# Expert layer with w1 as the stationary operand, its last three tiles under a branch, and the routing moved inside the attention's branch

## The chip, the cores and the metric

The kernel runs on one core of one Trainium2 chip. The metric is device time in microseconds (us) of one execution. The core has a TensorE (PE for its matmuls, PEld for its weight loads), a VectorE (DVE), a ScalarE (ACT), a GpSimd (POOL) and a SyncE (SP); each runs its own instruction stream in order, and they tell each other of finished work by semaphores. A TensorE instruction multiplies a stationary operand, which is loaded first, with a moving operand that streams past it, and writes to PSUM.

## The reference, cut to what matters

A recurrent attention block gives x, one row of 384 values for each of 3072 tokens. Each token is then sent to one of eight experts, a two-layer network.

```python
logits = x @ w_gate                      # x: 3072 x 384, 8 experts
expert_idx = np.argmax(logits, axis=1)
gate_w = probs[np.arange(N), expert_idx] # softmax of the logits
for e in range(E):
    mask = expert_idx == e
    xe = x[mask]
    h = np.maximum(xe @ w1[e], 0.0)      # w1[e]: 384 x 1024
    ye = h @ w2[e]                       # w2[e]: 1024 x 384
    out[mask] = gate_w[mask, None] * ye
```

All of it is fp32. The inputs are drawn from a fixed seed. Counted over these inputs, the experts get 380, 348, 359, 410, 409, 389, 374 and 403 tokens; in tiles of 128 tokens of one expert that is 3 + 3 + 3 + 4 + 4 + 4 + 3 + 4 = 28 tiles.

## The kernel before, in words

**Attention.** L558 is a branch on the decay weights: `fast()` (L335 to L552), which these inputs take, or `general()` (L126 to L332). At its end `fast()` gates the last batch: `gate_step` and `choose` (L104) make the logits, write x of that batch to the HBM buffer `x_hbm` with a DMA from SP (L124), and leave a one-hot row per token in `oh_all` (L122). The program text of `general()` lies between `fast()` and what comes after the branch.

**Routing**, L571 to L653, after the branch. Two matmuls (L573, L574) and a chain of small DVE operations, which starts with copies out of PSUM (`rk` L578, `cnt` L579), give each token its rank in its expert, the expert `ei` of each tile (L622), and `idx` (L653), the token numbers of each tile. The number of tiles isn't known when the program is built, so the kernel always runs NTILE = 24 + 8 - 1 = 31 tiles; tiles past the real number gather a row of zeros, and their scatter drops every row.

**Experts**, L658 to L725. For a tile j there are five steps, in an order that is written out by hand:

- `m_load(j)`: PE and SP load the expert's number into a register (L660), SP starts the DMA of `w1` of that expert (1536 KB, L663, three buffers), POOL starts the gather of the tile's rows `xs` from `x_hbm` (L665, four buffers).
- `m_xT(j)`: three TensorE transposes (L673) of `xs`, copied out by DVE to `xT` (L675).
- `m_h(j)`: for each half `fb` of the 1024 hidden units three matmuls of 512 moving columns: a block of `xT` is stationary, `w1` is moving (L683); ACT takes the ReLU to `h` (L685), tokens on partitions.
- `m_hT(j)`: eight transposes of `h` (L694), copied out by DVE in two halves to `hT` (L695), hidden units on partitions.
- `m_y(j)`: eight matmuls of 384 moving columns (L701): a block of `hT` is stationary, `w2` of the expert is moving; DVE scales by the gate weight (L704), POOL starts the scatter to `out` (L705).

An fp32 matmul shows up in the profile as two passes, each with its own weight load: six matmuls in `m_h` are 12 PE instructions, eight in `m_y` are 16. A transpose is one pass.

The loop (L715 to L725) issues, for each j: load(j+2), h(j), y(j-1), xT(j+1), hT(j). So y of a tile runs one iteration after its h.

Of the kernel before, what the change touches and what calls it, by code (L numbers as in the profile page):

```python
# [32 lines left out]
NTILE = NG + E - 1  # L33

# [6 lines left out]
def rwkv5_then_switch(ctx, tc, r, k, ktm, v, w, wl, u, wg, wgh, w1, w2, out):  # L41
# [511 lines left out]

    for e in range(E):
        nc.scalar.dma_start(w2_all[:, e, :], w2[e])
    usual = nc.values_load(wi[0:1, 0:1], min_val=0, max_val=1,
                           skip_runtime_bounds_check_because="a product of two comparisons")
    with tc.If(usual > 0) as which:  # L558
        fast()
    with which.Else():  # L560
        general()


    mo = ctx.enter_context(tc.tile_pool(name="mo", bufs=2))
    rt = ctx.enter_context(tc.tile_pool(name="rt", bufs=1))
    pm = ctx.enter_context(tc.tile_pool(name="pm", bufs=1, space=PSUM))

    def small(shape, nm, dt=FP32):
        return rt.tile(shape, dt, name=nm)

    rkp = pm.tile([128, 512], FP32, name="rkp", tag="y", bufs=2)  # L571
    oh_f = oh_all.rearrange("p g e -> p (g e)")
    nc.tensor.matmul(rkp[:, 0:NG * E], lhsT=Tmat, rhs=oh_f, start=True, stop=True, skip_group_check=True)  # L573
    nc.tensor.matmul(rkp[:, 256:256 + NG * E], lhsT=ones_bf, rhs=oh_f, start=True, stop=True,  # L574
                     skip_group_check=True)
    rk = small([128, NG, E], "rk")
    cnt = small([128, NG, E], "cnt")
    nc.vector.tensor_copy(rk.rearrange("p g e -> p (g e)"), rkp[:, 0:NG * E])  # L578
    nc.vector.tensor_copy(cnt.rearrange("p g e -> p (g e)"), rkp[:, 256:256 + NG * E])  # L579
    inc = cnt  # L580
    d = 1
    while d < NG:
        t = small([128, NG, E], f"inc{d}")
        nc.vector.tensor_copy(t[:, 0:d], inc[:, 0:d])
        nc.vector.tensor_tensor(t[:, d:], inc[:, d:], inc[:, :NG - d], op=ALU.add)
        inc = t
        d *= 2

    nc.vector.tensor_tensor(rk, rk, inc, op=ALU.add)
    nc.vector.tensor_tensor(rk, rk, cnt, op=ALU.subtract)  # L590
    nc.vector.tensor_tensor(rk, rk, oh_all, op=ALU.mult)
    rank = small([128, NG], "rank")
    nc.vector.tensor_reduce(rank, rk, axis=AX, op=ALU.add)
    rki = small([128, 3, NG], "rki", I32)
    nc.vector.tensor_copy(rki[:, 0, :], rank)
    nc.vector.tensor_scalar(out=rki[:, 1, :], in0=rki[:, 0, :], scalar1=127, scalar2=None, op0=ALU.bitwise_and)
    nc.vector.tensor_scalar(out=rki[:, 2, :], in0=rki[:, 0, :], scalar1=7, scalar2=None,
                            op0=ALU.logical_shift_right)
    rlh = small([128, 2, NG], "rlh")
    nc.vector.tensor_copy(rlh, rki[:, 1:3, :])  # L600

    ci = small([128, E], "ci", I32)
    nc.vector.tensor_scalar_add(ci, inc[:, NG - 1, :], 127.0)
    nc.vector.tensor_scalar(out=ci, in0=ci, scalar1=7, scalar2=None, op0=ALU.logical_shift_right)
    til = small([128, E], "til")
    nc.vector.tensor_copy(til, ci)
    last = til
    for d in (1, 2, 4):
        t = small([128, E], f"til{d}")
        nc.vector.tensor_copy(t[:, 0:d], last[:, 0:d])  # L610
        nc.vector.tensor_tensor(t[:, d:], last[:, d:], last[:, :E - d], op=ALU.add)
        last = t
    base = small([128, E], "base")
    nc.vector.tensor_tensor(base, last, til, op=ALU.subtract)

    tge = small([1, NTILE, E], "tge")
    nc.vector.tensor_tensor(tge, bc(iota_f[0:1, 0:NTILE, None], [1, NTILE, E]),
                            bc(last[0:1, None, :], [1, NTILE, E]), op=ALU.is_ge)
    ef = small([1, NTILE], "ef")
    nc.vector.tensor_reduce(ef, tge, axis=AX, op=ALU.add)  # L620
    ei = small([1, NTILE], "ei", I32)
    nc.vector.tensor_scalar_min(ei, ef, float(E - 1))  # L622

    nc.vector.tensor_tensor(rk, oh_all, bc(base[:, None, :], [128, NG, E]), op=ALU.mult)
    jt = small([128, NG], "jt")
    nc.vector.tensor_reduce(jt, rk, axis=AX, op=ALU.add)
    nc.vector.tensor_tensor(jt, jt, rlh[:, 1, :], op=ALU.add)

    At = small([128, NG, 128], "At", BF16)
    nc.vector.tensor_tensor(At, bc(iota_f[:, None, :], [128, NG, 128]),  # L630
                            bc(rlh[:, 0, :, None], [128, NG, 128]), op=ALU.is_equal)
    Bm = small([128, NG, NTILE], "Bm")
    nc.vector.tensor_tensor(Bm, bc(iota_f[:, None, 0:NTILE], [128, NG, NTILE]),
                            bc(jt[:, :, None], [128, NG, NTILE]), op=ALU.is_equal)
    hi_f = small([128, NG], "hi_f")
    nc.vector.tensor_scalar_add(hi_f, iota_f[:, 0:NG], 1.0)
    Bv = small([128, NG, 2, NTILE], "Bv", BF16)
    nc.vector.tensor_tensor(Bv[:, :, 0, :], Bm, bc(hi_f[:, :, None], [128, NG, NTILE]), op=ALU.mult)
    nc.vector.tensor_scalar_mul(Bv[:, :, 1, :], Bm, lo_f)
    idp = pm.tile([128, 2, NTILE], FP32, name="idp", tag="y", bufs=2)  # L640
    for g in range(NG):
        nc.tensor.matmul(idp.rearrange("p u j -> p (u j)"), lhsT=At[:, g, :],
                         rhs=Bv[:, g].rearrange("p u j -> p (u j)"), start=g == 0, stop=g == NG - 1)
    idl = small([128, 2, NTILE], "idl")
    nc.vector.tensor_copy(idl, idp)
    emp = small([128, NTILE], "emp")
    nc.vector.tensor_scalar(out=emp, in0=idl[:, 0, :], scalar1=0.0, scalar2=float(N + 128),
                            op0=ALU.is_equal, op1=ALU.mult)
    raw = small([128, NTILE], "raw")
    nc.vector.scalar_tensor_tensor(out=raw, in0=idl[:, 0, :], scalar=128.0, in1=idl[:, 1, :],  # L650
                                   op0=ALU.mult, op1=ALU.add)
    idx = small([128, NTILE], "idx", I32)
    nc.vector.scalar_tensor_tensor(out=idx, in0=raw, scalar=-128.0, in1=emp, op0=ALU.add, op1=ALU.add)  # L653


    mt = [dict() for _ in range(NTILE)]

    def m_load(j):  # L658
        m = mt[j]
        m["e"] = nc.values_load(ei[0:1, j:j + 1], engines=[ENG.PE, ENG.SP], min_val=0, max_val=E - 1,  # L660
                                skip_runtime_bounds_check_because="a count of at most E, cut to E - 1")
        m["w1"] = mo.tile([128, DT, F], FP32, name="w1s", bufs=3)
        nc.sync.dma_start(m["w1"], w1[ds(m["e"], 1)].rearrange("a p d f -> p (a d) f"))  # L663
        m["xs"] = mo.tile([128, W], FP32, name="xs", bufs=4)
        nc.gpsimd.indirect_dma_start(  # L665
            out=m["xs"], out_offset=None, in_=x_hbm[:, :],
            in_offset=bass.IndirectOffsetOnAxis(ap=idx[:, j:j + 1], axis=0))

    def m_xT(j):
        m = mt[j]  # L670
        p = pm.tile([128, DT, 128], FP32, name="xTp", tag="xT", bufs=1)
        for d in range(DT):
            nc.tensor.transpose(p[:, d, :], m["xs"][:, 128 * d:128 * d + 128], ident)  # L673
        m["xT"] = mo.tile([128, DT, 128], FP32, name="xT", bufs=2)
        nc.vector.tensor_copy(m["xT"], p)  # L675

    def m_h(j):
        m = mt[j]
        m["h"] = mo.tile([128, F], FP32, name="h", bufs=2)
        for fb in range(2):  # L680
            p = pm.tile([128, 512], FP32, name="hp", tag="h", bufs=3)
            for d in range(DT):
                nc.tensor.matmul(p, lhsT=m["xT"][:, d, :], rhs=m["w1"][:, d, fb * 512:(fb + 1) * 512],  # L683
                                 start=d == 0, stop=d == DT - 1)
            nc.scalar.activation(m["h"][:, fb * 512:(fb + 1) * 512], p, func=ACT.Relu)  # L685

    def m_hT(j):
        m = mt[j]
        m["hT"] = mo.tile([128, FT, 128], FP32, name="hT", bufs=2)
        for fb in range(2):  # L690
            p = pm.tile([128, 4, 128], FP32, name="hTp", tag="hT", bufs=2)
            for f in range(4):
                o = (4 * fb + f) * 128
                nc.tensor.transpose(p[:, f, :], m["h"][:, o:o + 128], ident)  # L694
            nc.vector.tensor_copy(m["hT"][:, 4 * fb:4 * fb + 4, :], p)  # L695

    def m_y(j):
        m = mt[j]
        p = pm.tile([128, DM], FP32, name="yp", tag="y", bufs=2)
# [11 lines left out]
    with tc.manual_schedule():  # L711
        for j in range(2):
            m_load(j)
        m_xT(0)
        for j in range(NTILE + 1):  # L715
            if j + 2 < NTILE:
                m_load(j + 2)
            if j < NTILE:
# [54 lines left out]
```

## Time and profile before

| | us |
|---|---|
| median of 3 runs | 602.97 (601.86 to 608.3) |
| the profiled execution, its own time | 607.18 |
| its span, first to last instruction | 605.5 |
| PE busy in the span | 516.7 |
| weight loads (PEld) busy | 340.0 |
| DVE, ACT, POOL busy | 182.5, 129.4, 161.0 |

The page also says that 96.48 MB went by DMA, 159 GB/s on average. Attention takes the first 204 us, routing some 30 us with TensorE nearly idle, the expert loop the rest. The mean duration of one PE instruction is longer than the distance between two, since matmuls are pipelined; the distance between starts is what a pass costs in a stream.

### The profile page before, as it was taken

The numbers are of one execution on the slowest core, as the hardware profiler recorded it, in microseconds if no ns is written. First come the engines' busy times: TensorE is split into PE (matmuls) and PEld (weight loads), VectorE is DVE, ScalarE is ACT, GpSimd is POOL, SyncE is SP. The second block draws the span as 40 slices with busy tenths as digits, with TensorE's granted clock in tenths as the row PEclk, the third lists the DMA queues.
The fourth block names the chain that finished last, engine by engine and source line by source line (L and its number), as shares of the span: only waits on it lengthen the run. The fifth ranks groups of instructions, "written<-read, shape, count | busy, mean of one in ns | idle before, by whom it ended". The sixth has DMA issues, their size and how long they took to land.

```text
span 605.5 us, 8757 instructions
## 1 busy us (share of the span) xinstructions
PE 516.7 (85%) x3223; PEld 340.0 (56%) x3223; DVE 182.5 (30%) x442; ACT 129.4 (21%) x379; POOL 161.0 (27%) x185
## 2 busy tenths in 40 slices
PE   0029898998997206999999999999999999999996
PEld 0028887998896202555555555555555555555553
DVE  6115767337443260211311221131122113112211
ACT  0026675445564000010011001001101100110110
POOL 5038875445560011111211121121112112111101
PEclk9999999569799556999999999999999999999999
DMA  7998654933922253645444544544454454455000
GB/s 263 355 335 206 170 147 123 208 79 110 210 54 79 84 232 133 224 141 206 159 152 162 203 145 145 206 148 150 169 186 153 145 192 161 145 175 191 29 0 0
DMA packets 22295, 96.48 MB, mean 159 GB/s; under 512 B 4352, under 2 KB 7462, under 8 KB 17252
## 3 DMA queue, kind: packets, MB, share of 16 engines
q1 hardware_dynamic: 17124, 72.40, 36.9%
q0 software_dynamic: 3968, 10.84, 5.7%
q10 hardware_dynamic: 1152, 12.58, 5.6%
q8 instruction: 29, 0.48, 0.3%
q14 instruction: 22, 0.18, 0.1%
HBM read 86.36 MB, written 10.83 MB: 161 GB/s over the span
## 4 chain that ended last, share of the span: by engine, by line
issue 57%; PE 19%; DMA 8%; POOL 7%; DVE 6%; ACT 3%; ACTq 0%; POOLq 0%; DVEq 0%; SPq 0%
DMA w_all<-in_moe_w_dram 6%; POOL xs L665 5%; PE rp L513 4%; PE P L447 4%; PE yp L504 3%; PE P L453 3%; PE yp L500 2%; POOL out_dram L705 2%; ACT A L461 2%; PE Gp L478 2%; DMA x_hbm<-xb 1%; DVE A L463 1%; DVE St L485 1%; DVE At L630 1%; DMA V<-in_v_dram 1%
## 5 line engine op out<-in xcount | busy, mean ns | idle before, releaser
L683 PE MATMUL hp<-w1s,xT 128*128 128x512 f32 x372 | 170.0, 607 | 0.7 <-DVE xT L675 0.7
L701 PE MATMUL yp<-w_all,hT 128*128 x496 | 165.1, 486 | 0.4 <-DVE hT L695 0.4
L701 PEld LDWEIGHTS yp<-w_all,hT 128*128 128x128 f32 x496 | 94.2, 190 | 72.5 <-issue 14.3
L683 PEld LDWEIGHTS hp<-w1s,xT 128*128 128x128 f32 x372 | 68.9, 192 | 82.7 <-issue 75.4
L705 POOL DMA_INDIRECT out_dram<-yo,idx x31 | 31.5, 1015 | 306.4 <-DVE yo L704 296.5
L685 ACT ACTIVATE h<-hp 128x512 f32<-128x512 f32 x62 | 37.0, 597 | 349.8 <-PE hp L683 349.8
L704 DVE TENSOR_SCALAR yo<-yp,xs 128x384 f32<-128x384 f32 x31 | 19.2, 618 | 289.4 <-PE yp L701 289.4
L461 ACT ACTIVATE A<-ident,dv 128x128 f32<-128x128 f32 x192 | 59.6, 389 | 0.1
L428 POOL TENSOR_TENSOR K<-kT,W 128x384 f32<-128x384 f32 x32 | 36.1, 1127 | 67.7 <-DMA kT<-in_k_dram 29.4
L463 DVE COPY_PREDICATED A<-mask,P 128x384 f32<-128x384 int32 x64 | 33.9, 583 | 57.2 <-ACT A L461 48.7
L447 PE MATMUL P<-R,K 48*128 48x128 f32 x384 | 35.2, 324 | 18.4 <-POOL K L428 14.3
L665 POOL DMA_INDIRECT xs<-x_hbm,idx x31 | 30.4, 980 | 55.5 <-issue 55.5
L504 PE MATMUL yp<-A,V 128*64 128x128 f32 x384 | 43.7, 305 | 1.2 <-DVE A L463 1.1
L447 PEld LDWEIGHTS P<-R,K 48*128 48x128 f32 x384 | 28.4, 218 | 23.6 <-POOL K L428 14.9
L695 DVE COPY hT<-hTp 128x512 f32<-128x512 f32 x62 | 39.6, 680 | 0.0
L500 PE MATMUL yp<-R,St 128*64 128x128 f32 x320 | 36.1, 306 | 0.0
L513 PE MATMUL rp<-IW,y 128*128 128x104 f32 x192 | 32.2, 319 | 4.0 <-DVE lg L516 4.0
L432 POOL TENSOR_TENSOR RK<-rT,kT 128x384 f32<-128x384 f32 x32 | 34.2, 1068 | 0.1
L513 PEld LDWEIGHTS rp<-IW,y 128*128 128x128 f32 x192 | 27.6, 222 | 8.8 <-DVE lg L516 4.9
L694 PE MATMUL hTp<-ident,h 128*128 128x128 f32 x248 | 32.3, 273 | 0.0
L504 PEld LDWEIGHTS yp<-A,V 128*64 128x64 f32 x384 | 27.9, 156 | 1.6 <-DVE A L463 1.6
L453 PEld LDWEIGHTS P<-wu,RK 48*128 48x128 f32 x384 | 28.7, 219 | 0.0
(111 smaller groups left out, 313.1 us busy)
## 6 DMA issues: line engine op xcount, KB each, us to landing
w1s<-in_moe_w_dram SPq DMA_DIRECT2D x31, 1536.0 KB, 6.4
w_all<-in_moe_w_dram ACTq DMA_DIRECT2D x8, 1536.0 KB, 20.0
x_hbm<-xb SPq DMA_DIRECT2D x4, 1155.0 KB, 5.8
rT<-in_r_dram SPq DMA_DIRECT2D x32, 144.0 KB, 3.9
kT<-in_k_dram SPq DMA_DIRECT2D x32, 144.0 KB, 3.9
kt<-in_k_tokens_dram SPq DMA_DIRECT2D x16, 288.0 KB, 4.7
V<-in_v_dram SPq DMA_DIRECT2D x16, 288.0 KB, 4.0
xs<-x_hbm,idx POOLq DMA_INDIRECT x31, 3.1
```

The costliest lines, as they stand in the source:

```text
L447: nc.tensor.matmul(P[hi][:, c * C:(c + 1) * C], lhsT=x["K"][q, c, :], rhs=x["R"][q, c, :], start=True, stop=True, skip_group_check=True)
L453: nc.tensor.matmul(P[hi][:, o:o + 1], lhsT=x["RK"][q, c * C:(c + 1) * C], rhs=wu[q, 1, hp:hp + 1], start=True, stop=True, skip_group_check ...
L461: nc.scalar.activation(A[:, hi, c, :], ident, func=ACT.Copy, scale=dv[:, hi, c:c + 1])
L463: nc.vector.copy_predicated(A[:, hi], bc(mask[:, None, :].bitcast(I32), [128, HC, C]), P[hi][:, 0:HC * C].rearrange("p (c t) -> p c t", c=HC))
L500: nc.tensor.matmul(yp[q, c, :], lhsT=m["St"][:, g, hi, :], rhs=x["R"][:, c, :], start=True, stop=False, skip_group_check=True)
L504: nc.tensor.matmul(yp[q, c, :], lhsT=vh(x, c, hi, 64), rhs=x["A"][:, hi, c, :], start=g == 0, stop=True, skip_group_check=True)
L513: nc.tensor.matmul(rp[:, hp, :], lhsT=pairs[b * HP + hp]["y"][:, ch * C:(ch + 1) * C], rhs=IW[:, hp, :], start=True, stop=True, skip_group ...
L665: nc.gpsimd.indirect_dma_start(out=m["xs"], out_offset=None, in_=x_hbm[:, :], in_offset=bass.IndirectOffsetOnAxis(ap=idx[:, j:j + 1], axis=0))
L683: nc.tensor.matmul(p, lhsT=m["xT"][:, d, :], rhs=m["w1"][:, d, fb * 512:(fb + 1) * 512], start=d == 0, stop=d == DT - 1)
L695: nc.vector.tensor_copy(m["hT"][:, 4 * fb:4 * fb + 4, :], p)
L701: nc.tensor.matmul(p, lhsT=m["hT"][:, f, :], rhs=w2_all[:, ds(m["e"], 1), f * DM:(f + 1) * DM], start=f == 0, stop=f == FT - 1)
L705: s_ = nc.gpsimd.indirect_dma_start(out=out[:, :], out_offset=bass.IndirectOffsetOnAxis(ap=idx[:, j:j + 1], axis=0), in_=y[:, :], in_offse ...
```

## The change

1. **w1 stationary.** In `m_h` a 128x128 block of `w1` is now the stationary operand and `xT` (128 columns) the moving one. The product comes out with hidden units on partitions, so the ReLU writes `hT` directly; `m_hT` is gone, and `h` with it. Three matmuls for each of eight blocks: 24 matmuls of 128 columns in place of 6 of 512.
2. **Order.** For each j: load(j+2), h(j), xT(j+1), y(j).
3. **Tile count.** NSURE = 24 + 4 = 28 tiles are run always; the other three lie under `tc.If(tiles > NSURE)`, where `tiles` is the real count, loaded into a register on each engine.
4. **Seam.** Routing and experts are a function `experts()` that is called inside each arm of the branch of L558, after `fast()` and after `general()`, not once behind it.

Cut to its core (the routing's lines move with no other change than `nt`):

```diff
+NSURE = NG + E // 2
...
+        nt = small([1, 1], "nt", I32)
+        nc.vector.tensor_copy(nt, last[0:1, E - 1:E])
...
+        tiles = nc.values_load(nt[0:1, 0:1], min_val=0, max_val=NTILE,
+                               skip_runtime_bounds_check_because="at most NTILE tiles by their count")
...
+        def m_h(j):
+            m = mt[j]
+            m["hT"] = mo.tile([128, FT, 128], FP32, name="hT", bufs=2)
+            for fb in range(2):
+                p = pm.tile([128, 4, 128], FP32, name="hp", tag="h", bufs=4)
+                for f in range(4):
+                    o = (4 * fb + f) * 128
+                    for d in range(DT):
+                        nc.tensor.matmul(p[:, f, :], lhsT=m["w1"][:, d, o:o + 128], rhs=m["xT"][:, d, :],
+                                         start=d == 0, stop=d == DT - 1)
+                nc.scalar.activation(m["hT"][:, 4 * fb:4 * fb + 4, :], p, func=ACT.Relu)
...
+        with tc.manual_schedule():
+            for j in range(2):
+                m_load(j)
+            m_xT(0)
+            for j in range(NSURE):
+                if j + 2 < NTILE:
+                    m_load(j + 2)
+                m_h(j)
+                if j + 1 < NTILE:
+                    m_xT(j + 1)
+                m_y(j)
+        with tc.If(tiles > NSURE):
+            with tc.manual_schedule():
+                for j in range(NSURE, NTILE):
...
     with tc.If(usual > 0) as which:
         fast()
+        experts()
     with which.Else():
         general()
...
+        experts()
...
-    def m_h(j):
-        m = mt[j]
-        m["h"] = mo.tile([128, F], FP32, name="h", bufs=2)
-        for fb in range(2):
-            p = pm.tile([128, 512], FP32, name="hp", tag="h", bufs=3)
-            for d in range(DT):
-                nc.tensor.matmul(p, lhsT=m["xT"][:, d, :], rhs=m["w1"][:, d, fb * 512:(fb + 1) * 512],
-                                 start=d == 0, stop=d == DT - 1)
-            nc.scalar.activation(m["h"][:, fb * 512:(fb + 1) * 512], p, func=ACT.Relu)
-
-    def m_hT(j):
...
-                nc.tensor.transpose(p[:, f, :], m["h"][:, o:o + 128], ident)
-            nc.vector.tensor_copy(m["hT"][:, 4 * fb:4 * fb + 4, :], p)
...
-        for j in range(NTILE + 1):
-            if j + 2 < NTILE:
-                m_load(j + 2)
-            if j < NTILE:
-                m_h(j)
-            if j > 0:
-                m_y(j - 1)
-            if j + 1 < NTILE:
-                m_xT(j + 1)
-            if j < NTILE:
-                m_hT(j)
```

## Rows read from the trace of the kernel before

**Rows 1.** The page's 40 slices of the span: PE busy, granted clock.
```profile
PE   0029898998997206999999999999999999999996
PEclk9999999569799556999999999999999999999999
```

**Rows 2.** The page's group of hT's transposes: count | busy us, mean ns | idle before.
```profile
L694 PE MATMUL hTp<-ident,h 128*128 128x128 f32 x248 | 32.3, 273 | 0.0
```

**Rows 3.** Windows of one expert tile: us, PE busy (instructions), clock, DMA share, GB/s.
```profile
242.64:247.86 5.22, 5.22 (x14) 1.00 0.68 275
247.86:253.02 5.16, 5.16 (x17) 1.00 0.79 288
253.02:254.36 1.34, 1.34 (x12) 1.00 0.16 64
254.36:583.42 329.06, 329.06 (x1094) 1.00 0.44 155
```

**Rows 4.** Timeline, PE and PEld, 128x128 blocks stationary: start us, us, what.
```profile
77.79 1.14 PE L513 MATMUL rp<-IW,y 128*128 128x104 f32 x8
77.79 0.97 PEld L513 LDWEIGHTS rp<-IW,y 128*128 128x128 f32 x8 [0.17 <-issue]
115.31 1.78 PEld L513 LDWEIGHTS rp<-IW,y 128*128 128x128 f32 x8 [0.33 <-issue]
253.35 1.04 PE L694 MATMUL hTp<-ident,h 128*128 128x128 f32 x8
78.86 0.94 PE L447 MATMUL P<-R,K 48*128 48x128 f32 x12
```

**Rows 5.** Line L513's weight loads: count, ns min/median/max, first to last start us.
```profile
L513 PEld LDWEIGHTS rp<-IW,y x192: 186/192/338, 77.8 to 200.6; 128*128 128x128 f32 x192
```

**Rows 6.** Timeline of the last tile's end.
```profile
594.57 1.28 DVE L695 COPY hT<-hTp 128x512 f32<-128x512 f32 x2
595.30 5.43 PE L701 MATMUL yp<-w_all,hT 128*128 x16 [0.43 <-DVE hT L695]
600.77 0.62 DVE L704 TENSOR_SCALAR yo<-yp,xs 128x384 f32<-128x384 f32 x1 [4.92 <-PE yp L701]
```

**Rows 7.** Timeline of ACT in the expert loop, one ReLU.
```profile
248.06 0.60 ACT L685 ACTIVATE h<-hp 128x512 f32<-128x512 f32 x1 [1.98 <-PE hp L683]
```

**Rows 8.** Timeline from the end of attention to the first expert matmuls.
```profile
203.71 0.21 DVE L122 TENSOR_TENSOR oh_all<-eq,m 128x48 bf16<-128x48 f32 x1
204.18 0.36 PE L574 MATMUL rkp<-oh_all,ones_bf 128*128 128x192 bf16 x1
209.58 0.36 DVE L578 COPY rk<-rkp 128x192 f32<-128x192 f32 x1 [5.66 <-DMA x_hbm<-xb]
...
225.23 1.18 POOL L665 DMA_INDIRECT xs<-x_hbm,idx  x1 [46.31 <-issue]
...
233.93 7.50 PE L683 MATMUL hp<-w1s,xT 128*128 128x512 f32 x12 [0.65 <-DVE xT L675]
```

**Rows 9.** Single lines' sequencer instructions: count, ns min/median/max, first to last start us.
```profile
L558 DVEq COMPARE_BRANCH  x2: 50/54/57, 4.3 to 203.7; - x2
L558 ACTq COMPARE_BRANCH  x2: 38/42/45, 11.3 to 202.5; - x2
L578 DVEq EVENT_SEMAPHORE  x5: 21/50/50, 207.8 to 209.5; - x5
L685 ACTq EVENT_SEMAPHORE  x5: 17/38/29463, 205.1 to 209.4; - x5
L769 POOLq DRAIN  x3: 45/113/3185, 601.4 to 605.2; - x3
L769 SPq DRAIN  x3: 7/7/13, 604.4 to 604.9; - x3
```

**Rows 10.** Windows, all engines: PE, PEld, DVE, ACT, POOL busy, clock, DMA, GB/s.
```profile
100.00:200.00 100.00, 89.75 (x1108) 82.58 (x1105) 47.95 (x136) 50.87 (x174) 41.54 (x45) 0.80 0.47 120
```

**Rows 11.** DMA issues: engine, operation, count, KB each, median us to landing.
```profile
w1s<-in_moe_w_dram SPq DMA_DIRECT2D x31, 1536.0 KB, 6.4
```

More of the change, by code (lines that the diff above doesn't have):

```diff
@@ L559, in rwkv5_then_switch @@
         fast()
+        experts()
     with which.Else():
         general()
[L564 to L652, printed above, removed]
@@ L653, in rwkv5_then_switch @@
-    nc.vector.scalar_tensor_tensor(out=idx, in0=raw, scalar=-128.0, in1=emp, op0=ALU.add, op1=ALU.add)
-    mt = [dict() for _ in range(NTILE)]
-    def m_load(j):
-        m = mt[j]
[L660 to L667, printed above, removed]
@@ L669, in m_xT @@
-    def m_xT(j):
-        m = mt[j]
-        p = pm.tile([128, DT, 128], FP32, name="xTp", tag="xT", bufs=1)
-        for d in range(DT):
-            nc.tensor.transpose(p[:, d, :], m["xs"][:, 128 * d:128 * d + 128], ident)
-        m["xT"] = mo.tile([128, DT, 128], FP32, name="xT", bufs=2)
-        nc.vector.tensor_copy(m["xT"], p)
-    def m_h(j):
-        m = mt[j]
-        m["h"] = mo.tile([128, F], FP32, name="h", bufs=2)
-        for fb in range(2):
-            p = pm.tile([128, 512], FP32, name="hp", tag="h", bufs=3)
-            for d in range(DT):
-                nc.tensor.matmul(p, lhsT=m["xT"][:, d, :], rhs=m["w1"][:, d, fb * 512:(fb + 1) * 512],
-                                 start=d == 0, stop=d == DT - 1)
-            nc.scalar.activation(m["h"][:, fb * 512:(fb + 1) * 512], p, func=ACT.Relu)
@@ L687, in m_hT @@
-    def m_hT(j):
[L688 to L693, printed above, removed]
-                nc.tensor.transpose(p[:, f, :], m["h"][:, o:o + 128], ident)
-            nc.vector.tensor_copy(m["hT"][:, 4 * fb:4 * fb + 4, :], p)
-    def m_y(j):
-        m = mt[j]
-        p = pm.tile([128, DM], FP32, name="yp", tag="y", bufs=2)
-        for f in range(FT):
-            nc.tensor.matmul(p, lhsT=m["hT"][:, f, :], rhs=w2_all[:, ds(m["e"], 1), f * DM:(f + 1) * DM],
-                             start=f == 0, stop=f == FT - 1)
-        y = mo.tile([128, DM], FP32, name="yo", bufs=3)
-        nc.vector.tensor_scalar_mul(y, p, m["xs"][:, DM:W])
-        s_ = nc.gpsimd.indirect_dma_start(
-            out=out[:, :], out_offset=bass.IndirectOffsetOnAxis(ap=idx[:, j:j + 1], axis=0),
-            in_=y[:, :], in_offset=None, bounds_check=N - 1, oob_is_err=False)
-        tc.declare_no_dep(s_.ins, group="sc", reason="each token stands in one tile: the rows are disjoint")
-        tc.add_to_no_dep_group("sc", s_.ins)
@@ L711, in rwkv5_then_switch @@
[L711 to L714, printed above, removed]
-        for j in range(NTILE + 1):
-            if j + 2 < NTILE:
-                m_load(j + 2)
-            if j < NTILE:
-                m_h(j)
-            if j > 0:
-                m_y(j - 1)
-            if j + 1 < NTILE:
-                m_xT(j + 1)
-            if j < NTILE:
-                m_hT(j)
+        experts()
 _INS = ['r', 'k', 'k:tokens', 'v', 'w', 'w:row', 'u', 'moe_w_gate', 'moe_w_gate:heads', 'moe_w1', 'moe_w2']
```

123 lines of the change are left out of this document (added).

## The prediction, as put on record

> **What bounds the kernel now.** I read the page's slices first [rows 1]: PE is busy at 0.9 and more from slice 16 on, at full clock, to the end; before it comes a hole of two slices (0 and 2) in which the routing runs. So there are two things to shorten: the expert loop, where PE is the limit, and the hole, where a chain on other engines is. The page's groups then show what in the loop could go: 248 transposes of `hT`, eight for each of 31 tiles, 32.3 us of PE, none of it idle time [rows 2]. The windows of one tile [rows 3] give its parts: h 5.22 us, y 5.16, the three xT and eight hT transposes with their boundary 1.34, in sum 11.72; the last row holds 28 tiles from h to h, 329.06 / 28 = 11.752 us each, PE busy all of it at clock 1.00. Thirty-one of these are 364.3 us of the 605.5 us span. No DMA, ACT or DVE time matters in the loop as long as it is under that.
>
> **h with w1 stationary.** The product is the same, and so is the number of moving columns: 12 passes of 512 before, 48 of 128 after. Before, a pass costs 5.22 / 12 = 0.435 us, so 128 columns are 0.109 us. What is new is a weight load for each 128 columns, not for each 512. The attention stage holds the nearest rows. In L513 each fp32 pass has its own 128x128 stationary block and 104 moving columns; at full clock eight loads take 0.97 us [rows 4], the last of them 0.192 [rows 5], so one pass follows another after (0.97 - 0.192) / 7 = 0.111 us. The 104 columns alone would take 0.109 x 104/128 = 0.089 and leave no room for a load beside them in series: load and moving operand overlap, and the load sets the pitch. The transposes with 128 moving columns [rows 2, 4] give (1.04 - 0.273) / 7 = 0.110. A group of eight L513 passes including the switch to the next line (77.79 to 78.86) takes 1.07 us: 0.18 us for the switch, which after the change comes once in 48 passes. I take 0.111: h costs 48 x 0.111 = 5.33 us, 0.11 more than before. The bounds are 0.109 (the columns alone) and, if nothing were hidden, 0.220 (a rival, below).
>
> The Trainium skill speaks against this edit: its page "TensorE: Matmul & The Clock Gate", Back-to-back issue gap, gives 81 ns for a load-and-matmul pair of 128 columns where the matmul alone would take 56. By that ratio a pass here would be an estimated 0.158 us, h 7.6, and the sum about 606 us, no gain. The rows of L513, 0.111, do not show that ratio.
>
> **hT gone.** Eight transposes leave PE. Of the 1.34 us of xT and hT [rows 3], 11 x 0.110 = 1.21 are transposes and 0.13 is a boundary wait. Three transposes, 0.33, stay. Two DVE copies a tile go too, worth nothing since DVE is covered by PE.
>
> **Tile period after.** h 5.33 + xT 0.33 + y 5.16 + 0.14 for boundaries (about what is lost now) = 10.96 us.
>
> **Order.** y(j) now follows its own h after only three transposes. The last ReLU of a tile starts 0.20 us after the next PE work starts (247.86 against 248.06) and takes 0.60 [rows 3, 7], so it ends 0.80 us after h; the transposes cover 0.33. But y begins with the blocks f = 0 to 3, which the first ReLU wrote some 2.6 us earlier, and these passes last 2.6 us. It needs that the halves of `hT` are waited for separately. They are: y of the last tile starts at 595.30, 0.73 after the two copies began, while the second runs on to 595.85 [rows 6]. Cost 0. If the cover were gone, see the first rival. xT(j+1) is copied by DVE under the 5.16 us of y. On POOL the gather of j+2 now stands ahead of the scatter of j, on SP only w1 loads stand; the gather's buffer was freed two tiles before. A w1 load needs 6.4 us [rows 11] and is issued as soon as h(j-1) is done, 3 x 10.96 - 5.3 = 27.5 us ahead of its use. PE's register load per tile is unchanged and runs ahead of the array.
>
> **Three tiles less.** The reference's own inputs make 28 tiles, and 28 > 28 is false: the branch skips the last three. Loop: 31 x 11.752 = 364.3 before, 28 x 10.96 = 306.9 after: -57.4. The drain of the last tile (y waits 0.43 for its own `hT` [rows 6]) goes: -0.4. The start stays: the first 12 passes take 7.50 us [rows 8], 2.3 over 5.22, because PE comes cold from the hole, and it will again. Two loads of w1 that nobody uses (tiles 28, 29) lie under the last two tiles.
>
> **Seam.** DVE's first routing copy starts at 209.58 after 5.66 idle us that end with the DMA of `x_hbm`, although its input is ready when L574 ends, 204.18 + 0.36 = 204.54 [rows 8]. The copy doesn't read `x_hbm`; it waits because it stands behind a branch. DVE also needs from 203.7 (branch) to 207.8 (next instruction) merely to get over the untaken arm, ACT from 202.5 to 205.1 [rows 9]. Inside the arm neither is left, so the copy starts near 204.6: -5.0. What is late next: the gather, which does read `x_hbm`, starts 15.65 us after the copy (225.23 against 209.58), so near 220.3, and the DMA has landed before 209.58 [rows 8]; so the whole chain to the first h (233.93) moves up. The bound on the other side is 0, if the copy's memory makes it wait for that DMA anyway. I take -5.0: nothing in the routing reads the batch being written. The new copy `nt` and a register load on DVE add 0.1 to 0.6 on this chain: +0.3.
>
> **End.** The jump goes to the end of the kernel. After its last work each engine must leave the skipped tiles and then the untaken arm: two jumps. One cost 2.6 us on ACT, 4.1 on DVE [rows 9]. Before, POOL reaches its final drain at 601.4 and the kernel's end is gated by SP's at 604.4: 3.0 us of cover [rows 9]. Two jumps of 2.6 to 4.1 come out at +2.2 to +5.2, one jump at 0 to +1.1. I take +2.2: by then no bulk transfer runs beside the jump, as under ACT's.
>
> **Sum.** -57.4 - 0.4 - 5.0 + 0.3 + 2.2 = -60.3. From the profiled execution's 607.2 that is 546.9 (span about 545). This execution lies 4.2 us over the median of 602.97; against the median I expect 542.7.
>
> **Rivals.**
> - *y waits for the whole ReLU.* Then PE stands 0.80 - 0.33 = 0.47 us in every tile, 28 x 0.47 = 13: 556. For it speaks only that the cover shrinks; rows 6 speak against it.
> - *Seam kept, two slow jumps.* +5.0 and +3.0: 551. The copy's wait may be one for memory; the two jumps may both cost DVE's 4.1.
> - *Loads partly uncovered.* The gain goes when a pass costs 60.3 / (28 x 48) = 0.045 us more, 0.156: two fifths of the load's 0.111 outside the moving operand. Then the time is 603, no change. For it: h doubles its weight loads' share to one per 128 columns, right at the load's own pitch. Against: L513 and the transposes [rows 4].
> - *Slower: loads in series.* If load and moving operand took turns on a full array, a pass would be 0.109 + 0.111 = 0.220, h 10.56, 28 x 5.23 = +146: 689. It decides for slower from 0.162 a pass on. For it speaks L447 [rows 4], whose pairs use 48 rows and might overlap only because they use different ones; against it L513, whose blocks use all 128 rows and still follow at 0.111. At half clock (115.31) the pitch is (1.78 - 0.338) / 7 = 0.206 [rows 4, 5]: a clock lost in the loop would do the same. It was 0.80 on average between 100 and 200 us, where PE was busy 89.75 of 100 us [rows 10], but 1.00 where PE has no holes [rows 3], and the change makes no hole. The Trainium skill states the series rule, "TensorE: Matmul & The Clock Gate", The mechanism: a weight load overlaps a running matmul only in another row group. By this rule the time would be near that 689; the rows of L513 contradict it.
> - *That the branch doesn't skip* needs 29 tiles; the nearest count is five tokens off a tile's edge (380, 389). Left out.
>
> **How the numbers follow.** Forecast 0.80, late ReLU 0.06, kept seam with slow jumps 0.05, partly uncovered 0.05, series or lost clock 0.04. The likeliest is 542.7. Its low end: a pass of 0.109 (-2.7), free jumps (-2.2), some 2 us between runs: 535. Upward the unknowns, seam +5.0, jumps +3.0, boundaries doubled 28 x 0.14 = 3.9, together reach 555, the late ReLU 556: I take 557. A measurement of this kernel tells about 1%, 6 us, from no change. Faster by more: 0.91; within 1%: 0.05; slower: 0.04.
>
> **What will show it.** h to h 10.96 us; 48 passes of h starting 0.111 apart; no idle PE before L701; `rk` starting near 204.6 and the first h near 229; 28 scatters; the last y ending near 538 and the span some 7 us behind it. The forecast is wrong if PE's distance between passes of h is over 0.12, if PE idles between xT and y, or if engines arrive at the final drain more than 9 us after the last y.

## The result, and the profile after

| | before | after |
|---|---|---|
| median, us | 602.41 (600.51 to 608.3) | 540.33 (538.75 to 544.0) |
| the profiled execution, us | 607.18 | 540.06 |
| its span, us | 605.5 | 538.3 |

The ratio is 0.8963, 95% interval 0.8886 to 0.904: 62.1 us less between the medians, where 60.3 were forecast. Medians in this document are over all runs of a kernel and ratios over the fast ones alone, since some runs are slow, one of e10's four by far (2575.64 us). The first view of the changed kernel is the page's slices, PE busy and granted clock; they answer to [rows 1].

```profile
PE   0027889899899730399999999999999999999994
PEclk9999999969889855599999999999999999999999
```

The picture is the same, the stretch at 0.9 is shorter; the hole is still there. The page's groups of the expert loop (line, operation, count | busy us, mean ns | idle before):

```profile
L685 PEld LDWEIGHTS hp<-xT,w1s 128*128 128x128 f32 x1344 | 155.8, 194 | 8.2 <-DVE xT L674 1.1
L685 PE MATMUL hp<-xT,w1s 128*128 128x128 f32 x1344 | 156.1, 277 | 0.6 <-DVE xT L674 0.6
L693 PE MATMUL yp<-w_all,hT 128*128 x448 | 149.1, 486 | 0.0
```

1344 passes are 28 tiles of 48, 448 are 28 of 16: the branch skipped three tiles. Idle before h is 0.6 us in all, at the first tile. The windows of one tile (us, PE busy (instructions), clock, DMA share, GB/s), which answer to [rows 3]: 26 periods, then h, xT and y of a late tile.

```profile
237.94:519.97 282.03, 282.03 (x1743) 1.00 0.52 180
509.13:514.48 5.35, 5.35 (x49) 1.00 0.27 81
514.48:514.81 0.33, 0.33 (x5) 1.00 0.26 33
514.81:519.97 5.16, 5.16 (x18) 1.00 0.85 294
```

282.03 / 26 = 10.847 us a tile against 11.752: h 5.35, xT 0.33, y 5.16, and nothing between them. The timeline of the seam (start us, us, what [idle before]) answers to [rows 8].

```profile
196.89 0.21 DVE L123 TENSOR_TENSOR oh_all<-eq,m 128x48 bf16<-128x48 f32 x1
197.29 0.37 PE L569 MATMUL rkp<-oh_all,ones_bf 128*128 128x192 bf16 x1
201.65 0.36 DVE L573 COPY rk<-rkp 128x192 f32<-128x192 f32 x1 [4.55 <-DMA x_hbm<-xb]
...
225.57 7.04 PE L685 MATMUL hp<-xT,w1s 128*128 128x128 f32 x48 [0.65 <-DVE xT L674]
...
531.02 0.62 DVE L696 TENSOR_SCALAR yo<-yp,xs 128x384 f32<-128x384 f32 x1 [4.61 <-PE yp L693]
```

The first routing copy still waits for the DMA of `x_hbm`, 4.55 us. That is a step of the prediction gone wrong. With the rows of before [rows 6, 8] the two spans divide like this, from the start of one named instruction to the next:

| stage | before | after | difference |
|---|---|---|---|
| attention, to the last `oh_all` | 203.71 | 196.89 | -6.82 |
| seam, to the copy `rk` | 5.87 | 4.76 | -1.11 |
| routing, to the first h | 24.35 | 23.92 | -0.43 |
| expert loop, to the last `yo` | 366.84 | 305.45 | -61.39 |
| end, to the end of the span | 4.73 | 7.28 | +2.55 |
| span | 605.5 | 538.3 | -67.2 |

The change doesn't touch attention, so -6.82 isn't its doing: the profiled execution of before was a long one, 4.8 us over its median, while in all eleven profiles of kernels that share this attention code the last `oh_all` ended between 196.2 and 199.2 us. Without that row the change is worth -60.4 us.

The end, in the sequencer's own instructions (count, ns min/median/max, first to last start us), answers to [rows 9]:

```profile
L652 DVEq TENSOR_LOAD <-nt x1: 323/323/323, 531.5 to 531.5; - x1
L714 DVEq COMPARE_BRANCH  x2: 47/60/72, 531.9 to 532.2; - x2
L714 POOLq COMPARE_BRANCH  x2: 38/46/53, 532.5 to 533.4; - x2
L778 DVEq DRAIN  x2: 10/34/58, 535.1 to 537.7; - x2
L778 POOLq DRAIN  x3: 45/107/1436, 536.0 to 538.0; - x3
L778 SPq DRAIN  x3: 7/7/13, 535.2 to 537.7; - x3
```

The count is loaded into the registers only here, behind the last tile. DVE passes the inner branch at 531.9 and the jump at 532.2, and is at its drain at 535.1. POOL passes the inner branch at 532.5 and the jump over the untaken arm at 533.4, and reaches its drain at 536.0. SP is at its first drain at 535.2, so POOL is the last.

### The profile page after: what moved, and what is told of

It is laid out like the page before. It is cut to its first block, busy times and chain, and to the rows that moved or that the text cites. A ratio compares the mean times of both kernels' runs of the same rounds, so it can differ in the third digit from the quotient of the medians.

```text
span 538.3 us, 9970 instructions
## 1 busy us (share of the span) xinstructions
PE 449.0 (83%) x3893; PEld 377.4 (70%) x3893; DVE 146.6 (27%) x376; ACT 125.5 (23%) x373; POOL 158.3 (29%) x181
## 4 chain that ended last, share of the span: by engine, by line
PE 70%; DMA 10%; issue 9%; DVE 6%; ACT 3%; POOL 1%; ACTq 1%; POOLq 0%; DVEq 0%; SPq 0%
PE hp L685 25%; PE yp L693 23%; DMA w_all<-in_moe_w_dram 7%; PE rp L514 5%; PE P L448 4%; PE yp L505 4%; PE P L454 3%; PE yp L501 3%; PE Gp L479 2%; ACT A L462 2%; PE xTp L672 2%; DMA xs<-x_hbm,idx 1%; DVE St L486 1%; DMA x_hbm<-xb 1%; DVE A L464 1%
## 5 line engine op out<-in xcount | busy, mean ns | idle before, releaser
L685 PEld LDWEIGHTS hp<-xT,w1s 128*128 128x128 f32 x1344 | 155.8, 194 | 8.2 <-DVE xT L674 1.1
L685 PE MATMUL hp<-xT,w1s 128*128 128x128 f32 x1344 | 156.1, 277 | 0.6 <-DVE xT L674 0.6
L693 PE MATMUL yp<-w_all,hT 128*128 x448 | 149.1, 486 | 0.0
L693 PEld LDWEIGHTS yp<-w_all,hT 128*128 128x128 f32 x448 | 83.0, 190 | 51.8
L687 ACT ACTIVATE hT<-hp 128x512 f32<-128x512 f32 x56 | 33.4, 597 | 296.8 <-PE hp L685 296.8
L697 POOL DMA_INDIRECT out_dram<-yo,idx x28 | 28.5, 1019 | 248.9 <-DVE yo L696 248.9
L674 DVE COPY xT<-xTp 128x384 f32<-128x384 f32 x29 | 16.2, 558 | 152.9 <-PE xTp L672 152.9
L696 DVE TENSOR_SCALAR yo<-yp,xs 128x384 f32<-128x384 f32 x28 | 17.3, 618 | 129.0 <-PE yp L693 129.0
L448 PE MATMUL P<-R,K 48*128 48x128 f32 x384 | 32.7, 307 | 19.2 <-POOL K L429 15.2
L448 PEld LDWEIGHTS P<-R,K 48*128 48x128 f32 x384 | 26.3, 204 | 24.1 <-POOL K L429 15.7
L431 DVE TENSOR_TENSOR R<-rT,W 128x384 f32<-128x384 f32 x32 | 23.5, 737 | 14.6 <-DMA rT<-in_r_dram 10.3
```

The costliest lines, as they stand in the source:

```text
L448: nc.tensor.matmul(P[hi][:, c * C:(c + 1) * C], lhsT=x["K"][q, c, :], rhs=x["R"][q, c, :], start=True, stop=True, skip_group_check=True)
L685: nc.tensor.matmul(p[:, f, :], lhsT=m["w1"][:, d, o:o + 128], rhs=m["xT"][:, d, :], start=d == 0, stop=d == DT - 1)
L687: nc.scalar.activation(m["hT"][:, 4 * fb:4 * fb + 4, :], p, func=ACT.Relu)
L693: nc.tensor.matmul(p, lhsT=m["hT"][:, f, :], rhs=w2_all[:, ds(m["e"], 1), f * DM:(f + 1) * DM], start=f == 0, stop=f == FT - 1)
```

## The experiments

Each of them is an edit of the changed kernel. "After the attention" below is the span less the end of the last `oh_all`, which leaves attention's own variation out: 341.2 us for the changed kernel, 401.6 before.

### Undoing the w1-stationary h: e4_x_stationary

```diff
-    # for each block f, each d: lhsT=w1[:, d, 128 columns], rhs=xT[:, d, :]; ReLU to hT
+    # for each half, each d: lhsT=xT[:, d, :], rhs=w1[:, d, 512 columns]; ReLU to h
+    # m_hT: eight transposes of h, two copies; order h(j), y(j-1), xT(j+1), hT(j)
```

> The changed kernel with the old h: a block of xT stationary, w1 moving, 12 passes of 512 columns, ReLU to h, eight transposes, two DVE copies, in the old order h(j), y(j-1), xT(j+1), hT(j); 28 tiles, branch and seam as changed. Theory: PE alone sets the period, so it is the old 11.75 instead of 10.84 us, 28 x 0.91 = 25.5 us more: about 566. Rival: w1 stationary gains by something else than the transposes, such as waits at the boundaries between tiles; then the period lies between.

Measured: 568.23 us median (ratio 0.9413, 0.9313 to 0.9513); after the attention 367.0. The window of one period:

```profile
305.61:317.36 11.75, 11.75 (x40) 1.00 0.46 164
```

The period is the old one to the hundredth, and 28 x (11.75 - 10.85) = 25.2 us, against the 25.8 measured. New h and new order together are worth that; PE has no idle time either way.

### Keeping w1 stationary, undoing the order: e8_old_order

```diff
             m_h(j)
+            if j > 0: m_y(j - 1)
             m_xT(j + 1)
-            m_y(j)
```

> The changed kernel with w1 stationary but the old order h(j), y(j-1), xT(j+1), and y of the last tile at the end. Theory: the order is worth nothing, PE waits for nothing either way: period 10.84 us, about 540, the end alike. Rival: the new order needs or gives something: a boundary wait of 0.1 us or more for the copy of xT(j+1), which now comes just before h(j+1) and takes 0.56 us: 28 x 0.6 = 17 us more.

Measured: 570.79 us median (ratio 0.945, 0.9371 to 0.953), 30 us slower than the changed kernel and no better than the old h. The timeline of one boundary, the period's window, and the waits of the loop (us in total, times, longest):

```profile
317.78 0.49 PE L672 MATMUL xTp<-ident,xs 128*128 128x128 f32 x3
317.99 0.62 DVE L696 TENSOR_SCALAR yo<-yp,xs 128x384 f32<-128x384 f32 x1 [10.88 <-PE yp L693]
318.52 0.55 DVE L674 COPY xT<-xTp 128x384 f32<-128x384 f32 x1
319.12 5.62 PE L685 MATMUL hp<-xT,w1s 128*128 128x128 f32 x48 [0.85 <-DVE xT L674]
```
```profile
307.16:319.12 11.96, 11.11 (x67) 1.00 0.47 160
```
```profile
PE hp L685 <- DVE xT L674: 22.0, 26, 0.8
```

My theory (the order is worth nothing) fell; the rival named the place and 0.6 us, it is 1.11. In the old order xT(j+1) comes just before h(j+1), and h needs DVE's copy of it: PE stands 0.85 us a tile. DVE adds to this, for it scales y first (317.99): its copy starts 0.74 us after the transposes, where in the changed kernel it takes 0.53 (514.48 to 515.01). Before the change the eight transposes of `hT` stood between them and covered that copy, all but 0.13 us of it. The new h takes the transposes away, and with them the cover: alone it makes the tile longer, 11.96 against 11.75 us.

### One step of that order moved back: e10_xT_ahead_of_y

```diff
             m_h(j)
+            m_xT(j + 1)
             if j > 0: m_y(j - 1)
-            m_xT(j + 1)
```

> The old order with one step moved: h(j), xT(j+1), y(j-1). y still runs one tile late, but DVE's copy of xT(j+1) has a whole y to hide under. Theory from e8: its 1.11 us a tile are the wait of h(j+1) for that copy, so the period returns to 10.85 us and the time to about 540. Rival: what costs in e8 is that y runs a tile late (its hT kept for two iterations, both buffers in use): then the period stays near 11.96.

Measured: 543.4 us median (ratio 0.9009, 0.8957 to 0.906), after the attention 342.5. From h to h it is again 10.85:

```profile
299.92 0.62 DVE L696 TENSOR_SCALAR yo<-yp,xs 128x384 f32<-128x384 f32 x1 [4.61 <-PE yp L693]
310.77 0.62 DVE L696 TENSOR_SCALAR yo<-yp,xs 128x384 f32<-128x384 f32 x1 [4.61 <-PE yp L693]
```

y runs a tile late here as in e8, so that costs nothing; xT behind y was the whole loss. Of the new order, "xT before y" is the part that counts.

### Taking y's cover away: e6_y_reversed

```diff
-    for f in range(FT):
+    for f in range(FT - 1, -1, -1):       # start and stop flags turned with it
```

> The changed kernel with the eight blocks of y taken from the last to the first, so that y begins with a block that the second ReLU has only just written: the cover of the first rival taken away. Theory: the ReLU ends 0.80 us after h, the transposes cover 0.33, PE idles about 0.5 us before each y: period 11.3 us, 28 x 0.47 = 13 us more, about 553. Rival: y waited for both halves all along (then nothing changes) or the wait is covered by other work on PE.

Measured: 558.2 us median (ratio 0.9259, 0.9185 to 0.9333), after the attention 359.9. In the timeline the second ReLU and the y behind it:

```profile
302.61 0.60 ACT L687 ACTIVATE hT<-hp 128x512 f32<-128x512 f32 x1 [2.02 <-PE hp L685]
303.26 5.43 PE L693 MATMUL yp<-w_all,hT 128*128 x16 [0.36 <-ACT hT L687]
```

y now starts 0.05 us after the ReLU's end, in every tile; the period is 11.47 us, 0.625 more, 28 x 0.625 = 17.5 us of the 18.7. The first rival's mechanism is real and is avoided only because y begins with the blocks of the first ReLU, which runs 2.6 us before the second. I had priced it at 0.47 a tile. PE stands 0.36 by the profile; the other 0.26 is overlap that the stop takes away: a transpose lasts 0.273 us where the next pass usually starts 0.109 after it, and the first pass of y takes 0.1 longer to the second.

### Half the moving columns: e7_half_columns

```diff
-    nc.tensor.matmul(p[:, f, :], lhsT=w1[:, d, o:o + 128], rhs=xT[:, d, :], ...)
+    n = 128 if d == 0 else 64
+    nc.tensor.matmul(p[:, f, 0:n], lhsT=w1[:, d, o:o + 128], rhs=xT[:, d, 0:n], ...)
```

> The changed kernel with 64 moving columns instead of 128 in two of the three passes pairs of each block of h (d = 1 and 2): the second half of each tile's tokens lacks these products. Load theory: the weight load sets the pitch of 0.111 us, so h stays at 5.35 us and the time at 540. Column theory: the 128 columns set it (0.107) and the load hides below; then 32 of 48 passes fall to about 0.055, h to 3.6 us, the time by 28 x 1.75 = 49 us to about 491. In series (the slower rival), a pass would fall by 0.053 in the same way.

Measured: 545.09 us median (ratio 0.9056, 0.9001 to 0.911), after the attention 344.7. Window of one h, and the period:

```profile
308.59:313.89 5.30, 5.30 (x49) 1.00 0.27 88
308.59:319.39 10.80, 10.80 (x68) 1.00 0.54 184
```

A third of the moving columns are gone and h went from 5.35 to 5.30 us. So the moving columns don't set the pitch, 5.35 / 48 = 0.1115 us, and run under what does: were load and moving operand in series, h would have lost 1.7 us. That it is the load is seen in the starts within one h of this run: the loads follow each other every 0.110 to 0.113 us throughout, while the matmuls between them start 0.057 to 0.165 us apart. It also says that in this form of h fewer tokens in a tile would save next to nothing, as far down as was tried. The time is even a little higher, because the first tile took 17.3 us to the second h instead of 12.4. The windows of that stretch, first of the changed kernel, then of this one:

```profile
225.60:231.00 5.40, 5.40 (x36) 0.73 0.00 0
231.00:236.00 5.00, 5.00 (x28) 1.00 0.47 143
```
```profile
226.50:232.00 5.50, 5.50 (x26) 0.50 0.00 0
232.00:237.00 5.00, 5.00 (x26) 0.50 0.00 0
```

In this run the granted clock stayed at its lower level (1.2 GHz) past the first 10 us of h; in the changed kernel it was back at 2.4 within the first 5.4. Why it came back later is not shown.

### All tiles, and none of the branch: e5_all31, e1_static28

```diff
 # e5: 31 tiles written out; e1: 28
-    for j in range(NSURE): ...
-    with tc.If(tiles > NSURE): ...
+    for j in range(31 or 28): ...
```

> The changed kernel with all 31 tiles written out, without a branch on the count. Theory: three tiles are worth 3 x 10.84 = 32.5 us, less the 2.5 us that the branch costs at the end: 30 us slower than the changed kernel, about 570. Rival: the tiles past the count are cheaper or dearer than the others (their gathers read one row of zeros 128 times, their scatters drop every row), so that a period among the last three differs from 10.84 us.

Measured: 573.06 us median (ratio 0.9532, 0.9465 to 0.9599), after the attention 373.5, so 32.3 us more. The loop is 33.5 us longer: three periods of 10.847 are 32.5 and the first tile is 1.3 slower, 13.70 us to the second h instead of 12.37, less 0.3 for the xT of tile 28, which the changed kernel makes and doesn't use. The last two tiles, both empty, start their h at 542.78 and 553.63, 10.85 apart: an empty tile costs PE as much as a full one.

> The changed kernel without the branch on the tile count: 28 tiles are written out, the count is not loaded, tiles 28 to 30 don't exist (their two loads of w1 neither). Theory: the skip itself is free in the loop and costs only at the end, where each engine loads the count and one long jump takes about 2.6 us; from the last y's end to the span's end 4.7 us instead of 7.2, the time about 537.8, loop period 10.84 us as before. Rival: the branch also slows the loop (register loads, two unneeded w1 loads, more code to fetch): then the period falls under 10.84 and the gain is more than 2.5 us.

Measured: 539.53 us median (ratio 0.8986, 0.8906 to 0.9066), after the attention 338.8, 2.4 less than with the branch. The last y is scaled here:

```profile
529.34 0.62 DVE L694 TENSOR_SCALAR yo<-yp,xs 128x384 f32<-128x384 f32 x1 [9.90 <-PE yp L691]
```

The loop is the same (period 10.847, 305.2 against 305.4 us); the end, to the span's 535.0, is 5.66 instead of 7.28 us. So the inner branch with its load of the count costs 1.6 us, and the jump over the untaken arm, which e1 still takes, some 0.9 over the 4.73 of before. I had expected both in one number, 2.6, and the end of e1 at 4.7. The other 0.8 us lies ahead of the end, 0.5 of it in the routing (23.44 us; the other runs have 23.2 to 24.5), and is not shown to be the branch's.

### The seam undone: e2_seam_out

```diff
     with tc.If(usual > 0) as which:
         fast()
-        experts()
     with which.Else():
         general()
-        experts()
+    experts()
```

> The changed kernel with the seam undone: routing and experts stand once, behind the attention's branch. Theory of the prediction: the first routing copy loses its wait only inside the arm, so this is slower by about 5 us at the seam and gains 2.6 us at the end, where the long jump is gone: about 543. Rival, read from the changed kernel's trace: the copy waits for the DMA of x_hbm inside the arm too (4.55 us idle), because the attention's closed buffers, of which that DMA reads one, have to be free; then the seam was worth only 0 to 1 us (the copy starts 5.7 instead of 4.6 us after oh_all), the end falls from 7.2 to about 4.7 us, and the time is 538 to 540, no slower.

Measured: 541.78 us median (ratio 0.8999, 0.8926 to 0.9073), after the attention 341.5 against 341.2: the same. The copy in the timeline:

```profile
204.85 0.36 DVE L573 COPY rk<-rkp 128x192 f32<-128x192 f32 x1 [5.70 <-DMA x_hbm<-xb]
```

It waits 5.70 us, as it did before [rows 8], so the move into the arm is worth 1.1 us here. The end, from this line to the span's 540.7, is 4.64 us instead of 7.28, which pays it back:

```profile
536.06 0.62 DVE L696 TENSOR_SCALAR yo<-yp,xs 128x384 f32<-128x384 f32 x1 [4.61 <-PE yp L693]
```

The remaining 1.8 us went to the first gather (0.6) and the first tile (13.59 us to the second h instead of 12.37). The prediction's theory asked for 5 us at this place.

### What the copy waits for: e3_xb_apart

```diff
-    gx[b] = (ap2.tile([128, G, W], FP32, name="xb"), ...)
+    gx[b] = (xbp.tile([128, G, W], FP32, name="xb"), ...)   # a pool that closes after experts()
```

> The changed kernel with the attention's buffer xb, which the DMA to x_hbm reads, in a pool of its own that stays open until the experts are done. Theory: the copy's wait is one for the memory of the attention's closed pools; with xb outside of them the copy follows the second routing matmul within 0.1 us, 0.5 to 0.7 us after oh_all instead of 4.55, and everything up to the first h moves up by about 4: time about 536. Rival: the copy waits for something else that ends at the same time (the matmul's own completion, another DMA), or the gather then waits for x_hbm, so that the first h starts no earlier after oh_all than 28.5 us.

Measured: 537.38 us median (ratio 0.8948, 0.8861 to 0.9035), after the attention 337.2, 4.0 less. The timeline of the seam:

```profile
197.47 0.21 DVE L123 TENSOR_TENSOR oh_all<-eq,m 128x48 bf16<-128x48 f32 x1
198.28 0.36 DVE L573 COPY rk<-rkp 128x192 f32<-128x192 f32 x1 [0.60 <-PE rkp L569]
```

Now the copy follows its matmul. `xb` moved to a pool that stays open, nothing else, and the wait is gone: it was one for memory that attention had used, and that the DMA was still reading. Whether `rk` lies on the bytes of `xb` itself, or a new tile has to wait for all that used the closed pool, the run doesn't tell. Nor does it make the move into the arm superfluous: in e2, with the seam outside, DVE was at its next instruction only 4.0 us after its branch (199.0 to 202.9), so there the copy could hardly have started as early as 0.8 us behind `oh_all`. No run has `xb` apart and the seam outside. The medians alone, 537.38 against 540.33, don't tell the two kernels apart; the stages do.

### The version that the runs point to: e9_xb_apart_early_count

```diff
 # e3, and:
-        tiles = nc.values_load(nt[0:1, 0:1], ...)      # scheduled behind the loop
         with tc.manual_schedule():
+            tiles = nc.values_load(nt[0:1, 0:1], ...)
             for j in range(2):
                 m_load(j)
```

> The version that the runs point to: the changed kernel with xb in a pool of its own (as in e3, 4.0 us up to the first h) and the tile count loaded into the registers before the loop, not at its end. Theory: at the end DVE and POOL no longer load the count between their last work and the branch (0.3 us and its waits of 0.1 us each), so the end falls from 7.28 to about 6.5 us; span less the end of oh_all 336.5 us against 341.2, time about 536. Rival: the early loads delay the routing's chain (idx to first h over 9 us) and give back what the end gains.

Measured: 537.36 us median (534.71 to 541.02), ratio to the kernel before 0.893 (0.8895 to 0.8966). After the attention 336.5 us, as worked out. The copy again follows its matmul:

```profile
197.75 0.21 DVE L123 TENSOR_TENSOR oh_all<-eq,m 128x48 bf16<-128x48 f32 x1
198.56 0.36 DVE L573 COPY rk<-rkp 128x192 f32<-128x192 f32 x1 [0.60 <-PE rkp L569]
```

The end is 6.78 us (527.72 to the span's 534.5), and `idx` to the first h 8.8 us, no longer than in e3 (9.1). By the spans it is 4.7 us ahead of the changed kernel; the times alone, 537.36 against 540.33 with intervals that overlap, don't tell the two apart.

## Why the prediction was right, point by point

- **The total, -60.3 forecast, -60.4 in the stages the change touches, -62.1 between the medians.** It is partly luck: the seam was put some 3 us too large and the loop 3.6 us too small.
- **h with w1 stationary** [rows 4, 5]: right. 0.111 us a pass was read from L513, 5.33 us for h; it is 5.35. That the load sets the pitch was read from the same rows and is shown by e7. The loop shows neither of the two rivals with loads in the open: 48 different full-height blocks follow each other at 0.1115 us. Nor does it show the two rules of the Trainium skill's page "TensorE: Matmul & The Clock Gate" that the prediction cited for them (Back-to-back issue gap, The mechanism). One slip in the working: with 6 us for "slower", that rival decides from 0.111 + 66.3 / 1344 = 0.160 a pass on, not 0.162; no number of the forecast hangs on it.
- **Tile period, 10.96 forecast:** 0.11 too long. The term at fault is the 0.14 us for boundaries. It was carried over from the old loop, where it was the rest of DVE's copy of xT that the transposes left uncovered [rows 3]; the new order covers it wholly. 28 x 0.11 = 3.2 us, and with a shorter start of the first tile (the first h takes 7.04 us, 7.50 before) the loop gave 61.4 instead of 57.8.
- **Order, cost 0:** right for y (e6 shows the cover at work and its price of 17.5 us), but the prediction asked only what the new order might cost, not what the old one would. e8 answers: without the reorder the new h loses, 11.96 us a tile. Where I wrote of xT(j+1) "copied under the 5.16 us of y", the sentence held 31 us of the result and had no price beside it.
- **Three tiles less:** right; 3 x 10.847 = 32.5 us, and e5 gives 32.3 for skipping them, branch included.
- **Seam, -5.0:** wrong. The step that failed is "It waits because it stands behind a branch". The profile named the releaser, the DMA of `x_hbm` [rows 8], and I took the branch for the reason that it was waited for. The other bound, "if the copy's memory makes it wait for that DMA anyway", is what happened (e2, e3). The move gave 1.1, and 0.4 in the routing.
- **End, +2.2:** 2.55. The size is right, the make-up isn't, so that is partly luck too. The prediction took two long jumps less 3.0 us of cover. Of the two jumps only the one over the untaken arm is long (533.4 to 536.0 on POOL, 2.6 us as ACT's in [rows 9]). The inner branch and the load of the count in front of it, which the prediction placed in the routing's chain at +0.3, take 1.6 us together (e1). And the cover is smaller than 3.0: the inner branch alone shows nothing at the end (e2, 4.64 us), the jump alone 0.9 (e1), both 2.55; 2.6 + 1.6 - 2.55 leaves some 1.6 us of it, an estimate from these runs. Loading the count early takes 0.5 back (e9).

## What to carry to other kernels

When a change removes work from the engine that is the limit, ask what that work covered: here eight transposes hid a copy, and without moving another step the faster form is slower. Price the order as a part of its own, in both directions. And where a wait's releaser is a DMA that the waiting instruction doesn't read, look for shared memory before control flow: a buffer that a late DMA still reads belongs in a pool that isn't reused at once.

## What the runs showed of the hardware that was not expected

An fp32 pass with its own 128x128 block takes 0.1115 us from one to the next at full clock whether 128 or, in two of three, 64 columns move (e7), so at 128 columns load and moving operand are nearly level (by y's passes of 384 columns, 5.16 / 16 = 0.3225 us, 128 columns alone are 0.1075). In the same run the clock came back from 1.2 to 2.4 GHz more than 5 us later than in the changed kernel. And two taken branches of the same kernel cost very differently: over three tiles 0.3 us between DVE's two branch instructions (531.9 and 532.2), over the untaken arm 2.6 on POOL and 2.9 on DVE (drain at 535.1).
